# Gated linear attention with a gated MLP: transposes from TensorE to VectorE and DMA, value products on two column halves

## Chip, cores, metric

One core of one Trainium2 chip. The metric is the device time of one execution in microseconds (us), median of three runs.

## The reference, cut to what matters

Two blocks in float32 (the MLP's weights arrive as float64 and are converted on the chip). B = 4, H = 8, S = 768, D = 48; 3072 tokens of 384; the MLP is 2048 wide.

```python
mag = np.sqrt(a_re * a_re + a_im * a_im)
scale = np.minimum(mag, 0.999) / (mag + 1e-06)
a_re_n, a_im_n = (a_re * scale, a_im * scale)
for t in range(S):
    ar, ai = (a_re_n[:, :, t, :, None], a_im_n[:, :, t, :, None])
    new_re = ar * S_re - ai * S_im
    new_im = ar * S_im + ai * S_re
    kv = np.einsum('bhd,bhe->bhde', k[:, :, t], v[:, :, t])
    S_re, S_im = (new_re + kv, new_im)
    y[:, :, t] = np.einsum('bhd,bhde->bhe', q[:, :, t], S_re)
x = y.transpose(0, 2, 1, 3).reshape(B * S, H * D)
h = x @ w_in
return (h * np.cos(h)) @ w_out
```

## The kernel before

The complex gates are turned into magnitudes and angles, both summed along a chunk, so that a chunk's outputs are products of matrices. A chunk is C = 128 tokens of one batch (24 chunks, n), a group is G = 2 chunks (12 groups, g). All of it runs in `fast_path`; `general_path` stands behind a flag computed at the end and is not taken with these inputs.

Per group, on tiles of 128 tokens x 768 (two chunks x 8 heads x 48):

- `g_log` (L627), `g_prod` (L655), `g_angle` (L681): logarithm of the gate's magnitude (`m2`, called m in the trace), its running sum on TensorE (`lgs`, L662), the factors P and Q, and the angle. The last token's row of P goes to DRAM and comes back transposed as `end` (L674 to L675, two DMAs on SP's queue).
- `g_phase` (L693, `phs`), `g_trig` (L706): the running angle, its sine and cosine (`trig`).
- `g_stack` (L715): `ks` and `qs`, keys and queries times cosine and sine, 16 heads x 96 (L722, one VectorE operation of 128x1536 each).

Per chunk:

- `f_transpose` (L727): `kT` and `qT` [96, 8 heads, 128], eight TensorE transposes each (`tp`, L734), copied from PSUM by ScalarE (L736).
- `f_scores` (L738): per head kT x qT (`sc`, L744), multiplied on VectorE with the causal mask into `atm` (L746).
- `f_state` (L763): the chunk's own state, ks x v (`sp`, L769), added to the running `state` [96, 8, 48] by VectorE and GpSimd (L774 to L778); the last chunk of a batch has none.
- `f_out` (L749): `yp` = atm x v (L755) plus state x queries (L758; the first chunk of a batch has no state), tokens on partitions, copied to `x` (L761).
- `f_xt` (L782): x transposed by three TensorE transposes (`xp`, L788) into the group's `xT` (L789).

Per group again: `mm1` (L791), eight calls of twelve records on TensorE for two slices of the width (`hp`, L796), ScalarE and VectorE between (`turn`, `cs`, Sin), and the product `gate` (L807); `mm2` (L810), two calls of 16 matmuls (`op`, L813), then out. In the profile one float32 matmul counts as two records, a transpose as one.

The loop at the end of `fast_path` runs a software pipeline. Iteration `it` does the gates of group `it`, the chunks of `it-1`, `mm1` of `it-2` and `mm2` of `it-3`: first g_log, g_prod, g_angle and mm2, then a weave of the steps of `gates` (spread over the first half), `chunks` and `mm1` (spread over all of it). The Tile framework's scheduler takes this order as priorities, sets the final order on each engine and inserts the waits; buffers come from pools with a fixed number of copies (`bufs`). DMAs issued with `nc.sync` stand on one queue (SP) in order. `special` keeps the ScalarE functions that need a table in the order written, so the logarithms of the next group stand behind the last Sin of mm1.

Of the kernel before, what the change touches and what calls it, by code (L numbers as in the profile page):

```python
# [11 lines left out]
F32 = mybir.dt.float32  # L12
# [5 lines left out]
ALU = mybir.AluOpType  # L18
# [467 lines left out]
def fast_path(ctx, tc, q, k, v, a_re, a_im, moe_w_in, moe_w_out, out, least):  # L486
# [14 lines left out]
    ND = DM // C  # L501
    NJ = DF // C
    assert DM == H * D and NCH % G == 0

# [26 lines left out]
    X = [dict() for _ in range(NG)]  # L531
# [43 lines left out]
    def from_double(dst, src):  # L575
# [24 lines left out]
        nc.vector.scalar_tensor_tensor(out=dst, in0=e, scalar=897.0, in1=dst,  # L600
                                       op0=ALU.is_ge, op1=ALU.mult)

    chained = []

    def chain(ins):
# [18 lines left out]
    def temp(tag, bufs=1):  # L624
        return gt.tile([C, G * DM], F32, tag=tag, name=tag, bufs=bufs)
# [29 lines left out]
    def g_prod(g):  # L655


        x = X[g]
        x["P"], x["Q"] = temp("P"), temp("Q")
        for i in range(G):  # L660
            ps = pa.tile([C, DM], F32, tag="a", name="lgs")
            nc.tensor.matmul(ps, lhsT=sums, rhs=x["lg"][:, ts(i, DM)], start=True, stop=True)  # L662
            special(out=x["P"][:, ts(i, DM)], in_=ps, func=AF.Exp)
            special(out=x["Q"][:, ts(i, DM)], in_=ps, func=AF.Exp, scale=-1.0)
        u = temp("mag")
        nc.vector.scalar_tensor_tensor(out=u, in0=x["Q"], scalar=HUGE, in1=x["P"],
                                       op0=ALU.min, op1=ALU.mult)
        for name in "PQ":
            nc.vector.scalar_tensor_tensor(out=x[name], in0=u, scalar=3.0, in1=x[name],
                                           op0=ALU.subtract, op1=ALU.mult)  # L670
        row = rows_d.tile([G * DM], F32, tag="row", name="row")
        nc.scalar.dma_start(out=row, in_=x["P"][C - 1:C].rearrange("o x -> (o x)"))
        x["end"] = ft.tile([D2, G * H], F32, tag="end", name="end")
        for a in range(2):  # L674
            nc.sync.dma_start(out=x["end"][ds(a * D, D)], in_=row.rearrange("(x d) -> d x", d=D))  # L675
# [29 lines left out]

    def g_trig(g):  # L706
        x = X[g]
        x["trig"] = gt.tile([C, 2, G * DM], F32, tag="trig", name="trig")
        cs, sn = x["trig"][:, 0], x["trig"][:, 1]
        nc.vector.tensor_scalar(out=cs.bitcast(U32), in0=x["ph"].bitcast(U32),  # L710
                                scalar1=0x7FFFFFFF, scalar2=None, op0=ALU.bitwise_and)
        special(out=sn, in_=x["ph"], func=AF.Sin, scale=TWO_PI)
        special(out=cs, in_=cs, func=AF.Sin, scale=-TWO_PI, bias=half_pi_b)

    def g_stack(g):  # L715
        x = X[g]
        nc.gpsimd.tensor_tensor(out=x["P"], in0=flat(x["q"]), in1=x["P"], op=ALU.mult)
        nc.gpsimd.tensor_tensor(out=x["Q"], in0=flat(x["k"]), in1=x["Q"], op=ALU.mult)
        for name, src, eng in (("ks", x["Q"], nc.vector), ("qs", x["P"], nc.vector)):
            t = gt.tile([C, G * H, 2, D], F32, tag=name, name=name, bufs=2)  # L720
            shape = [C, G * H, 2, D]
            eng.tensor_tensor(  # L722
                out=t, in0=src.rearrange("p (x d) -> p x d", d=D).unsqueeze(2).to_broadcast(shape),
                in1=x["trig"].rearrange("p a (x d) -> p x a d", d=D), op=ALU.mult)
            x[name] = t

    def f_transpose(n, name, hh):  # L727
        g, i = divmod(n, G)
        if hh == 0:
            Y[n][name] = ft.tile([D2, H, C], F32, tag=name, name=name)  # L730
        ps = pa.tile([D2, HH, C], F32, tag="a", name="tp")
        for h in range(HH):
            head = i * H + hh * HH + h
            nc.tensor.transpose(ps[:, h], X[g][name[0] + "s"][:, head].rearrange(  # L734
                "p a d -> p (a d)"), ident)
        nc.scalar.copy(out=Y[n][name][:, ts(hh, HH)], in_=ps)  # L736

    def f_scores(n, hh):  # L738
        y = Y[n]
        if hh == 0:  # L740
            y["atm"] = ft.tile([C, H, C], F32, tag="atm", name="atm")
        ps = pa.tile([C, HH, C], F32, tag="a", name="sc")
        for h in range(HH):
            nc.tensor.matmul(ps[:, h], lhsT=y["kT"][:, hh * HH + h], rhs=y["qT"][:, hh * HH + h],  # L744
                             start=True, stop=True)
        nc.vector.tensor_tensor(out=y["atm"][:, ts(hh, HH)], in0=ps,  # L746
                                in1=causal.unsqueeze(1).to_broadcast([C, HH, C]), op=ALU.mult)

    def f_out(n):  # L749
        y, (g, i) = Y[n], divmod(n, G)  # L750
        vals = X[g]["v"][:, i]
        state = y.get("state")
        ps = pa.tile([C, H, D], F32, tag="a", name="yp")
        for h in range(H):
            nc.tensor.matmul(ps[:, h], lhsT=y["atm"][:, h], rhs=vals[:, h],  # L755
                             start=True, stop=(state is None))
            if state is not None:
                nc.tensor.matmul(ps[:, h], lhsT=y["qT"][:, h], rhs=state[:, h],  # L758
                                 start=False, stop=True)
        y["x"] = ft.tile([C, DM], F32, tag="x", name="x")  # L760
        nc.scalar.copy(out=y["x"], in_=ps.rearrange("p h d -> p (h d)"))  # L761

    def f_state(n):  # L763
        if n % NCH == NCH - 1:
            return
        y, (g, i) = Y[n], divmod(n, G)
        ps = pa.tile([D2, H, D], F32, tag="a", name="sp")
        for h in range(H):
            nc.tensor.matmul(ps[:, h], lhsT=X[g]["ks"][:, i * H + h].rearrange("p a d -> p (a d)"),  # L769
                             rhs=X[g]["v"][:, i, h], start=True, stop=True)  # L770
# [11 lines left out]
    def f_xt(n):  # L782
        g, i = divmod(n, G)
        if i == 0:
            X[g]["xT"] = msb.tile([C, ND, G, C], F32, tag="xT", name="xT")
        ps = pa.tile([C, ND, C], F32, tag="a", name="xp")
        for dc in range(ND):
            nc.tensor.transpose(ps[:, dc], Y[n]["x"][:, ts(dc, C)], ident)  # L788
        nc.scalar.copy(out=X[g]["xT"][:, :, i], in_=ps)  # L789

    def mm1(g, jp):  # L791
        x = X[g]
# [136 lines left out]
```

## Time and profile before

| | |
|---|---|
| median of 3 runs | 931.01 us (930.38 to 933.06) |
| the profiled execution | 938.23 us |
| its span | 936.4 us |
| instructions | 10169 |
| TensorE busy | 797.1 us, 85% of the span |
| VectorE busy | 497.1 us, 53% |
| ScalarE busy | 378.6 us, 40% |
| GpSimd busy | 171.3 us, 18% |

How to read the lines shown later. PE is TensorE's matmul stream, PEld its weight loads, DVE is VectorE, ACT ScalarE, POOL GpSimd, SP the engine that issues most DMAs; SPq is its queue. A row of groups gives the line, engine and operation, output and inputs by name, partitions x elements, how many; behind the first bar the busy time in us and the mean of one in ns; behind the second the idle time of the engine just before them and what ended most of it. A row of the chain of waits gives the start, the length and the work, one piece behind the other, each released by the one before. A row of windows gives the stretch, its length, the busy time and count of each engine in it, the granted TensorE clock (1.00 is full speed), the share of the DMA engines, and GB/s. A row of an engine's timeline gives start, length and operation.

### The profile page before, as it was taken

How to read it: one execution, taken by the hardware profiler on the slowest of the kernel's cores; microseconds unless marked ns; L12 is line 12 of the kernel's file. 1: busy time of each engine (PE TensorE's matmuls, PEld its weight loads, DVE VectorE, ACT ScalarE, POOL GpSimd, SP SyncE). 2: the span in 40 equal slices, each digit the busy share in tenths (PEclk: the TensorE clock that was granted, in tenths of full speed). 3: DMA queues.
4: the chain of work that ended last, by engine and by line, in shares of the span. 5: the costliest groups of instructions: out<-in, count | busy, mean ns of one | idle time of the engine just before them, and what ended most of it. 6: DMA issues, size and time to landing. Idle time of an engine off the chain costs nothing.

```text
span 936.4 us, 10169 instructions
## 1 busy us (share of the span) xinstructions
PE 797.1 (85%) x3920; PEld 621.0 (66%) x3920; DVE 497.1 (53%) x761; ACT 378.6 (40%) x588; POOL 171.3 (18%) x96
## 2 busy tenths in 40 slices
PE   1101446899999999999999999999999989999997
PEld 0000245685885977967968858858769668778684
DVE  3999985844544736636545446346456445123160
ACT  5222123535454554454364454354544623123140
POOL 2343333403103022112120031031030211000000
PEclk9999966899899999989899999898999998998999
DMA  8523631303004004004023040040040100000000
GB/s 174 141 90 112 146 108 34 69 18 63 23 18 85 1 18 85 1 17 85 1 43 60 18 83 3 18 85 1 18 84 1 26 10 1 9 9 1 9 8 21
DMA packets 151876, 42.03 MB, mean 45 GB/s; under 512 B 144638, under 2 KB 148222, under 8 KB 151818
## 3 DMA queue, kind: packets, MB, share of 16 engines
q1 hardware_dynamic: 151218, 40.98, 19.8%
q8 instruction: 33, 0.54, 0.3%
q10 hardware_dynamic: 600, 0.30, 0.1%
q14 instruction: 25, 0.20, 0.1%
HBM read 36.51 MB, written 4.76 MB: 44 GB/s over the span
## 4 chain that ended last, share of the span: by engine, by line
PE 70%; ACT 6%; DVE 2%; POOL 2%; DMA 1%; issue 1%; ACTq 0%; SPq 0%; POOLq 0%; DVEq 0%
PE hp L796 28%; PE op L813 17%; PE yp L755 4%; PE sc L744 4%; PE yp L758 4%; PE tp L734 4%; PE sp L769 3%; POOL m L646 2%; ACT rs L619 2%; PE lgs L662 1%; ACT L618 1%; PE phs L697 1%; PE phs L700 1%; PE xp L788 1%; ACT m L619 1%; ACT mag L619 1%
## 5 line engine op out<-in xcount | busy, mean ns | idle before, releaser
L796 PE MATMUL hp<-xT,w_in 128*128 128x256 f32 x1152 | 294.0, 409 | 4.1 <-DVE gate L807 3.5
L796 PEld LDWEIGHTS hp<-xT,w_in 128*128 128x128 f32 x1152 | 231.0, 207 | 39.7 <-DVE gate L807 3.9
L813 PE MATMUL op<-w_out,gate 128*128 128x384 f32 x768 | 251.1, 486 | 0.0
L813 PEld LDWEIGHTS op<-w_out,gate 128*128 128x128 f32 x768 | 145.9, 190 | 99.2
L803 DVE TENSOR_SCALAR cs<-turn 128x512 f32<-128x512 f32 x96 | 42.4, 443 | 172.9 <-ACT turn L802 172.9
L802 ACT ACTIVATE turn<-hp,quarter_b 128x512 f32<-128x512 f32 x96 | 65.7, 685 | 124.6 <-PE hp L796 122.7
L807 DVE TENSOR_TENSOR gate<-hp,cs 128x512 f32<-128x512 f32 x96 | 66.2, 690 | 82.2 <-ACT cs L619 81.4
L776 POOL TENSOR_TENSOR state<-state,end 96x384 f32<-96x384 f32 x16 | 31.2, 1949 | 342.2 <-DVE state L774 179.1
L755 PE MATMUL yp<-v,atm 128*128 128x48 f32 x384 | 75.3, 292 | 19.3 <-DVE atm L746 19.3
L619 ACT ACTIVATE cs<-cs 128x512 f32<-128x512 f32 x96 | 60.5, 630 | 69.0 <-DVE cs L805 69.0
L662 PE MATMUL lgs<-m,sums 128*128 128x384 f32 x48 | 21.3, 572 | 64.6 <-POOL m L646 49.3
L755 PEld LDWEIGHTS yp<-v,atm 128*128 128x128 f32 x384 | 62.0, 209 | 20.4 <-DVE atm L746 20.2
L758 PE MATMUL yp<-state,qT 96*128 96x48 f32 x320 | 67.7, 296 | 0.0
L805 DVE TENSOR_TENSOR cs<-turn,cs 128x512 f32<-128x512 f32 x96 | 65.9, 687 | 2.1
L662 PEld LDWEIGHTS lgs<-m,sums 128*128 128x128 f32 x48 | 9.2, 211 | 75.2 <-POOL m L646 71.3
L646 POOL TENSOR_TENSOR m<-m,rs 128x768 f32<-128x768 f32 x12 | 22.0, 1835 | 197.6 <-ACT rs L619 196.7
L697 PE MATMUL phs<-sq,sums 128*128 128x384 f32 x48 | 22.4, 557 | 38.8 <-DVE sq L688 38.8
L758 PEld LDWEIGHTS yp<-state,qT 96*128 96x128 f32 x320 | 54.2, 212 | 0.0
L761 ACT COPY x<-yp 128x384 f32<-128x384 f32 x24 | 11.5, 478 | 104.6 <-PE yp L758 94.0
L633 ACT ACTIVATE m<-re 128x768 f32<-128x768 f32 x12 | 10.1, 842 | 97.3 <-DMA re<-in_a_re_dram 97.3
L744 PE MATMUL sc<-qT,kT 96*128 96x128 f32 x384 | 48.4, 277 | 0.1
L744 PEld LDWEIGHTS sc<-qT,kT 96*128 96x128 f32 x384 | 46.9, 192 | 2.3 <-ACT qT L736 1.0
(77 smaller groups left out, 955.0 us busy)
## 6 DMA issues: line engine op xcount, KB each, us to landing
raw<-in_moe_w_in_dram SPq DMA_DIRECT2D x12, 512.0 KB
raw<-in_moe_w_out_dram SPq DMA_DIRECT2D x16, 384.0 KB
re<-in_a_re_dram SPq DMA_DIRECT2D x24, 192.0 KB
im<-in_a_im_dram SPq DMA_DIRECT2D x24, 192.0 KB
k<-in_k_dram SPq DMA_DIRECT2D x24, 192.0 KB
q<-in_q_dram SPq DMA_DIRECT2D x24, 192.0 KB
v<-in_v_dram SPq DMA_DIRECT2D x24, 192.0 KB
out_dram<-ot SPq DMA_DIRECT2D x24, 192.0 KB
```

The source lines that it names most:

```text
L619: chain(nc.scalar.activation(func=func, **kw))
L646: nc.gpsimd.tensor_tensor(out=m2, in0=m2, in1=rs, op=ALU.subtract)
L662: nc.tensor.matmul(ps, lhsT=sums, rhs=x["lg"][:, ts(i, DM)], start=True, stop=True)
L744: nc.tensor.matmul(ps[:, h], lhsT=y["kT"][:, hh * HH + h], rhs=y["qT"][:, hh * HH + h], start=True, stop=True)
L755: nc.tensor.matmul(ps[:, h], lhsT=y["atm"][:, h], rhs=vals[:, h], start=True, stop=(state is None))
L758: nc.tensor.matmul(ps[:, h], lhsT=y["qT"][:, h], rhs=state[:, h], start=False, stop=True)
L796: nc.tensor.matmul(ps[:, ji], lhsT=w_in[:, dc, ts(jp * 2 + ji, C)], rhs=x["xT"][:, dc].rearrange("p g t -> p (g t)"), start=(dc == 0), sto ...
L802: nc.scalar.activation(out=turn, in_=ps, func=AF.Identity, scale=INV_TWO_PI, bias=quarter_b)
L803: nc.vector.tensor_scalar(out=cs, in0=turn, scalar1=ROUND, scalar2=ROUND, op0=ALU.add, op1=ALU.subtract)
L805: nc.vector.tensor_tensor(out=cs, in0=turn, in1=cs, op=ALU.subtract)
L807: nc.vector.tensor_tensor(out=gate, in0=ps, in1=cs, op=ALU.mult)
L813: nc.tensor.matmul(ps, lhsT=X[g]["gate"][j // 2][:, j % 2, ts(i, C)], rhs=w_out[:, j], start=(j == 0), stop=(j == NJ - 1))
```

## The change

Four things, and no other arithmetic:

1. Keys and queries are no longer transposed on TensorE. VectorE transposes blocks of 32x32 (`tr` [128, 768], one operation for a chunk's keys, one for its queries, two buffers), and twelve DMAs on SP's queue put the blocks in place: four quarters of the tokens x three blocks of 32 rows, 32 partitions each. This step moves from `chunks(it-1)` to `gates(it)`, an iteration ahead of its use; kT and qT get three buffers. For blocks of 32 the 96 rows of a head are ordered in runs of 16 (cosine and sine alternately), so `ks` and `qs` are made by two VectorE operations of 128x768 each, `trig` lies in two temporaries that the next group uses as well, and `end` comes by six DMAs instead of two.
2. `f_out` computes the transpose of what it computed: v and state are the stationary operand (48 columns), atm and qT move (128 columns). Even heads go to PSUM partitions 0 to 47, odd heads to 64 to 111, in turn. Two ScalarE copies put the result into `yT`.
3. `f_xt` runs once per group: ten DMAs on SP's queue from yT to xT, in place of six TensorE transposes and two ScalarE copies.
4. `cs` shares the buffer of `gate`, of which there are eleven instead of twelve.

```diff
@@ g_prod
-        for a in range(2):
-            nc.sync.dma_start(out=x["end"][ds(a * D, D)], in_=row.rearrange("(x d) -> d x", d=D))
+        for part in range(D2 // R):
+            nc.sync.dma_start(
+                out=x["end"][ds(part * R, R)],
+                in_=row.rearrange("(x b d) -> b d x", d=R, b=NR)[part // 2])
@@ g_trig
-        x["trig"] = gt.tile([C, 2, G * DM], F32, tag="trig", name="trig")
-        cs, sn = x["trig"][:, 0], x["trig"][:, 1]
+        cs, sn = x["trig"] = temp("rs"), temp("mag")
@@ g_stack
+            t = gt.tile([C, G * H * NR, 2, R], F32, tag=name, name=name,
+                        bufs=2 if name == "ks" else 1)
+            for a in range(2):
+                nc.vector.tensor_tensor(
+                    out=t[:, :, a], in0=src.rearrange("p (x d) -> p x d", d=R),
+                    in1=x["trig"][a].rearrange("p (x d) -> p x d", d=R), op=ALU.mult)
@@ f_transpose
-        ps = pa.tile([D2, HH, C], F32, tag="a", name="tp")
-        for h in range(HH):
-            head = i * H + hh * HH + h
-            nc.tensor.transpose(ps[:, h], X[g][name[0] + "s"][:, head].rearrange(
-                "p a d -> p (a d)"), ident)
-        nc.scalar.copy(out=Y[n][name][:, ts(hh, HH)], in_=ps)
+        tr = ft.tile([C, NR, H, 32], F32, tag="tr", name="tr")
+        nc.vector.transpose(out=tr, in_=X[g][name[0] + "s"][:, ts(i, H * NR)].rearrange(
+            "p (h b) a d -> p b h (a d)", b=NR))
+        if name == "kT":
+            t = Y[n][name] = ft.tile([D2, H, Q4, 32], F32, tag=name, name=name, bufs=3)
+            place = t.rearrange("p h q j -> p q h j")
+        else:
+            t = Y[n][name] = place = ft.tile([D2, Q4, H, 32], F32, tag=name, name=name, bufs=3)
+        for a in range(Q4):
+            for b in range(NR):
+                nc.sync.dma_start(out=place[ts(b, 32), a], in_=tr[ts(a, 32), b])
@@ f_out
-        ps = pa.tile([C, H, D], F32, tag="a", name="yp")
-        for h in range(H):
-            nc.tensor.matmul(ps[:, h], lhsT=y["atm"][:, h], rhs=vals[:, h],
-                             start=True, stop=(state is None))
+        ps = pa.tile([C, HH, C], F32, tag="a", name="yp")
+        for p in range(HH):
+            for side in range(2):
+                nc.tensor.matmul(ps[ds(side * 64, D), p], lhsT=vals[:, 2 * p + side],
+                                 rhs=y["atm"][:, 2 * p + side], start=True, stop=(state is None))
             if state is not None:
-                nc.tensor.matmul(ps[:, h], lhsT=y["qT"][:, h], rhs=state[:, h],
-                                 start=False, stop=True)
-        y["x"] = ft.tile([C, DM], F32, tag="x", name="x")
-        nc.scalar.copy(out=y["x"], in_=ps.rearrange("p h d -> p (h d)"))
+                for side in range(2):
+                    nc.tensor.matmul(ps[ds(side * 64, D), p], lhsT=state[:, 2 * p + side],
+                                     rhs=queries(y, 2 * p + side), start=False, stop=True)
+        for side in range(2):
+            half = ds(side * 64, D)
+            nc.scalar.copy(out=X[g]["yT"][half, :, i], in_=ps[half])
@@ f_xt
-        ps = pa.tile([C, ND, C], F32, tag="a", name="xp")
-        for dc in range(ND):
-            nc.tensor.transpose(ps[:, dc], Y[n]["x"][:, ts(dc, C)], ident)
-        nc.scalar.copy(out=X[g]["xT"][:, :, i], in_=ps)
+        for h in range(H):
+            row = h * D
+            while row < (h + 1) * D:
+                n = min((h + 1) * D, (row // C + 1) * C) - row
+                nc.sync.dma_start(out=xt[ds(row % C, n), row // C],
+                                  in_=X[g]["yT"][ds(h % 2 * 64 + row - h * D, n), h // 2])
+                row += n
@@ mm1
-        cs = msb.tile([C, 2, G * C], F32, tag="cs", name="cs")
-        gate = msb.tile([C, 2, G * C], F32, tag="gate", name="gate", bufs=12)
+        gate = msb.tile([C, 2, G * C], F32, tag="gate", name="gate", bufs=11)
+        cs = gate
@@ gates
+        for i in range(G):
+            for name in ("kT", "qT"):
+                yield lambda i=i, name=name: f_transpose(g * G + i, name)
@@ chunks
-            for name in ("kT", "qT"):
-                for hh in range(2):
-                    yield lambda n=n, name=name, hh=hh: f_transpose(n, name, hh)
...
-            yield lambda n=n: f_xt(n)
+            if n == ns[-1]:
+                yield lambda: f_xt(g)
```

The new line numbers: hp L817, op L834, sc L758, sp L789, yp L772 (values) and L776 (state), tr L738, the DMAs of kT and qT L747, of xT L808, of end L679.

TensorE's order around the second chunk of a group, before (a program's matmul is one row here):

```order
L796 MATMUL hp<-xT,w_in 128x256 x6
L788 MATMUL xp<-ident,x 128x128 x3
L734 MATMUL tp<-ident,ks 96x128 x8
L796 MATMUL hp<-xT,w_in 128x256 x6
L734 MATMUL tp<-ident,qs 96x128 x8
L796 MATMUL hp<-xT,w_in 128x256 x6
L744 MATMUL sc<-qT,kT 128x128 x8
L796 MATMUL hp<-xT,w_in 128x256 x6
L769 MATMUL sp<-v,ks 96x48 x8
L755 MATMUL yp<-v,atm 128x48
L758 MATMUL yp<-state,qT 128x48
```

The same place now:

```order
L758 MATMUL sc<-qT,kT 128x128 x4
L817 MATMUL hp<-xT,w_in 128x256 x6
L758 MATMUL sc<-qT,kT 128x128 x4
L817 MATMUL hp<-xT,w_in 128x256 x6
L789 MATMUL sp<-v,ks 96x48 x8
L817 MATMUL hp<-xT,w_in 128x256 x6
L772 MATMUL yp<-atm,v 48x128 x2
L776 MATMUL yp<-qT,state 48x128 x2
```

The tp and xp are gone, and the sp, which stood directly ahead of yp, has a block of hp behind it now.

SP's queue over one group in the steady part of the loop, before:

```order
L541 DMA re<-in_a_re_dram 128x8x48
L675 DMA end<-row 48x16x1 x2
L541 DMA re<-in_a_re_dram 128x8x48
L541 DMA k<-in_k_dram 128x8x48
L541 DMA q<-in_q_dram 128x8x48 x2
L817 DMA out_dram<-ot 128x384
L541 DMA v<-in_v_dram 128x8x48 x2
```

And now:

```order
L544 DMA q<-in_q_dram 128x8x48 x2
L747 DMA kT<-tr 32x8x32 x12
L747 DMA qT<-tr 32x256 x12
L747 DMA kT<-tr 32x8x32 x12
L747 DMA qT<-tr 32x256 x12
L808 DMA xT<-yT 48x256 x2
L808 DMA xT<-yT 32x256
L808 DMA xT<-yT 16x256
L808 DMA xT<-yT 48x256 x2
L808 DMA xT<-yT 16x256
L808 DMA xT<-yT 32x256
L808 DMA xT<-yT 48x256 x2
```

The 48 DMAs of the next group's kT and qT stand ahead of the ten that make this group's xT.

VectorE's order in the start-up now, from the last part of the weight conversion (L603) on; the tr up to here are group 0's and group 1's:

```order
L603 SCALAR_TENSOR_TENSOR w_out<-t,w_out 128x384
L738 STREAM_TRANSPOSE tr<-qs 128x768
L760 TENSOR_TENSOR atm<-sc,causal 128x512 x2
L793 SCALAR_TENSOR_TENSOR state<-sp,state 96x384
L639 TENSOR_TENSOR m_824<-m_824,sq 128x768
L644 TENSOR_TENSOR mag<-mag,sq 128x768
L645 TENSOR_SCALAR m_824<-m_824 128x768
L738 STREAM_TRANSPOSE tr<-ks 128x768
L653 SCALAR_TENSOR_TENSOR sq<-mag,sq 128x768
L655 SCALAR_TENSOR_TENSOR sq<-sq,im 128x768
L670 SCALAR_TENSOR_TENSOR mag<-Q,P 128x768
L673 SCALAR_TENSOR_TENSOR P<-mag,P 128x768
```

Two more operations of g_prod follow, with the last transpose of group 1 between them: what belongs to group 2's gates (L639 to L673) stands among group 1's transposes.

More of the change, by code (lines that the diff above doesn't have):

```diff
@@ L501, in fast_path @@
     ND = DM // C
+    R = 16
+    NR = D // R
+    Q4 = C // 32
     NJ = DF // C
@@ L718, in g_stack, with f_transpose, queries @@
         nc.gpsimd.tensor_tensor(out=x["Q"], in0=flat(x["k"]), in1=x["Q"], op=ALU.mult)
[L719 to L724, printed above, removed]
+        for name, src in (("ks", x["Q"]), ("qs", x["P"])):
+            t = gt.tile([C, G * H * NR, 2, R], F32, tag=name, name=name,
[4 more added lines that the diff above has]
+                    in1=x["trig"][a].rearrange("p (x d) -> p x d", d=R), op=ALU.mult)
             x[name] = t
-    def f_transpose(n, name, hh):
+    def f_transpose(n, name):
         g, i = divmod(n, G)
-        if hh == 0:
-            Y[n][name] = ft.tile([D2, H, C], F32, tag=name, name=name)
-        ps = pa.tile([D2, HH, C], F32, tag="a", name="tp")
-        for h in range(HH):
-            head = i * H + hh * HH + h
-            nc.tensor.transpose(ps[:, h], X[g][name[0] + "s"][:, head].rearrange(
-                "p a d -> p (a d)"), ident)
-        nc.scalar.copy(out=Y[n][name][:, ts(hh, HH)], in_=ps)
+        tr = ft.tile([C, NR, H, 32], F32, tag="tr", name="tr")
[9 more added lines that the diff above has]
+                nc.sync.dma_start(out=place[ts(b, 32), a], in_=tr[ts(a, 32), b])
+    def queries(y, h):
+        return y["qT"][:, :, h]
     def f_scores(n, hh):
@@ L768, in f_state @@
         for h in range(H):
-            nc.tensor.matmul(ps[:, h], lhsT=X[g]["ks"][:, i * H + h].rearrange("p a d -> p (a d)"),
-                             rhs=X[g]["v"][:, i, h], start=True, stop=True)
+            keys = X[g]["ks"][:, ts(i * H + h, NR)].rearrange("p b a d -> p (b a d)")
+            nc.tensor.matmul(ps[:, h], lhsT=keys, rhs=X[g]["v"][:, i, h], start=True, stop=True)
         new = ft.tile([D2, H, D], F32, tag="state", name="state")
@@ L780, in f_state, with f_xt @@
         Y[n + 1]["state"] = new
[L782 to L785, printed above, removed]
-        ps = pa.tile([C, ND, C], F32, tag="a", name="xp")
-        for dc in range(ND):
-            nc.tensor.transpose(ps[:, dc], Y[n]["x"][:, ts(dc, C)], ident)
-        nc.scalar.copy(out=X[g]["xT"][:, :, i], in_=ps)
+    def f_xt(g):
+        xt = X[g]["xT"] = msb.tile([C, ND, G, C], F32, tag="xT", name="xT")
+        for h in range(H):
[5 more added lines that the diff above has]
+                row += n
     def mm1(g, jp):
```

4 lines of the change are left out of this document (3 added, 1 removed).

## The prediction

> **What bounds the kernel now.** First the page's totals, its chain by engine, and one stretch from the first op (L813) to the last op's end beside the stretch before it.
>
> ```profile
> span 936.4 us, 10169 instructions
> PE 797.1 (85%) x3920; PEld 621.0 (66%) x3920; DVE 497.1 (53%) x761; ACT 378.6 (40%) x588; POOL 171.3 (18%) x96
> PE 70%; ACT 6%; DVE 2%; POOL 2%; DMA 1%; issue 1%; ACTq 0%; SPq 0%; POOLq 0%; DVEq 0%
> ```
> ```profile
> core 0: us, PE busy (x) PEld busy (x) DVE busy (x) ACT busy (x) POOL busy (x), PEclk, DMA share, GB/s
> 0.00:209.40 209.40, 89.35 (x447) 71.50 (x448) 158.06 (x265) 68.12 (x98) 70.64 (x47) 0.89 0.41 99
> 209.40:930.45 721.05, 707.79 (x3474) 549.53 (x3472) 339.06 (x496) 309.98 (x489) 100.69 (x49) 0.96 0.14 29
> 482.14:544.70 62.56, 61.37 (x323) 48.06 (x323) 33.95 (x49) 31.37 (x49) 9.52 (x6) 1.00 0.20 39
> 544.70:614.07 69.37, 68.18 (x338) 53.63 (x338) 34.04 (x49) 31.31 (x49) 12.45 (x7) 0.93 0.17 35
> ```
> From 209.4 to 930.45 PE is busy for 707.79 of 721.05 us: PE is the bound there, and what is taken off it comes off the time. Before 209.4 VectorE is the busiest (158.06 of 209.4, most of it converting weights). The granted clock is 0.96 in the long stretch, so about 0.04 x 721 = 29 us are lost to it. The last two rows are two groups with the same kinds of work: one at clock 1.00, the other at 0.93 and 6.8 us longer.
>
> Then the places where the clock goes: the chain of waits around two chunks, and windows cut at its pieces.
>
> ```profile
> 443.53 1.32 PE sp L769 x16
> 444.85 0.22 PE yp L755 x2
> 445.07 0.22 PE yp L758 x2
> ...
> 509.84 1.32 PE sp L769 x16
> 511.16 1.79 PE yp L755 x16
> ```
> ```profile
> 443.53:447.40 3.87, 3.87 (x41) 3.87 (x40) 3.54 (x5) 0.80 (x2) 0.85 (x1) 0.98 0.01 4
> 447.40:449.40 2.00, 2.00 (x11) 2.00 (x11) 1.28 (x1) 0.01 (x1) 1.97 (x1) 0.50 0.00 0
> 449.40:451.00 1.60, 1.60 (x5) 1.24 (x6) 0.57 (x1) 1.00 (x2) 0.00 (x0) 0.50 0.00 0
> ...
> 509.84:512.95 3.11, 3.11 (x33) 3.11 (x33) 2.78 (x4) 0.80 (x2) 0.00 (x0) 1.00 0.00 0
> 512.95:515.00 2.05, 2.05 (x10) 1.80 (x10) 2.05 (x3) 1.07 (x2) 0.00 (x0) 1.00 0.00 0
> ```
> At 443.53 the products of 48 moving columns begin, sp and then sixteen yp in one run; 3.9 us later the clock is 0.50, though PE is busy in every microsecond. At 509.84 the chunk has no state, the run of such products ends after 3.11 us, and the clock stays at 1.00. So it is not idle time that halves the clock here but a long run of thin products. The Trainium skill ("TensorE: Matmul & The Clock Gate", what's actually happening) gives half rate after an idle window of about 3.4 us. By that rule nothing in this change would touch the 29 us and the sum below would be 25 us smaller; the trace, halved with PE busy 2.00 of 2.00 us, speaks against idleness as the cause.
>
> **The change part by part.** I count from the first op on, where ten of the twelve groups still have their chunk work to do, and against the profiled run (936.4 plus 1.8 around it = 938.23 us, 7.2 above the median of 931.01).
>
> *Transposes off PE.* The rows are pieces of the chain at full clock.
>
> ```profile
> 454.42 0.33 PE xp L788 x3
> 454.75 0.87 PE tp L734 x8
> ...
> 439.15 1.79 PE sc L744 x16
> ```
> A tp takes 0.87/8 = 0.109 us; ten groups have 320: -34.9 us. An xp takes 0.11, ten groups have 60: -6.5. The ACT copies of both (L736, L789) go too, but ACT is busy 31 of 62 to 69 us per group, so that counts nothing.
>
> *Value and state products.* Before, a product is 0.22 us for a pair of records with the whole array as weights and 48 columns moving. Now 48 columns are the weights, 128 move, and two neighbours stand in different column halves. The ten groups have 160 value and 136 state products: 296 x 0.2235 = 66.2 us. No row shows two halves at work together. If they overlap fully, half goes: -33.1. If they don't, a product costs what another one with 128 moving columns does, sc: 1.79/8 = 0.224 us, thus no gain, with some loss for changing the array's form. I take the overlap, as independent outputs on separate columns have nothing in common but the moving side, less 0.25 us at each of the 20 chunks for the change of form, 5 us, an estimate of the size of one product's time: -28. Ends: -33 and +5. The Trainium skill ("TensorEngine Tiling (Array Packing)", Key Properties) says that tiles run in parallel and that a change of tiling mode drains the array; no row here shows either.
>
> *The clock.* sp and yp now have a hp of 2.6 us at full rate between them, and yp's run is shorter and moves 128 columns, as sc does at clock 1.00. I take 25 of the 29 us as regained; ends 0 and 29.
>
> *What comes instead: VectorE.* Four 32x32 transposes of 128x768 per group. The trace has none; the nearest row has the same shape, and ks and qs (L722) are split into ops of half the size.
>
> ```profile
> L635 DVE TENSOR_TENSOR m<-m,sq 128x768 f32<-128x768 f32 x12 | 11.4, 948 | 7.2 <-ACT sq L634 7.2
> L722 DVE TENSOR_TENSOR qs<-P,trig 128x1536 f32<-128x1536 f32 x12 | 22.1, 1839 | 0.0
> L813 PE MATMUL op<-w_out,gate 128*128 128x384 f32 x768 | 251.1, 486 | 0.0
> ```
> 0.95 us each, 3.8 per group: VectorE goes from 34.0 to 37.8 us of a group that I expect to last 65.6 - 9 = 57. Of that, some 30 lie in the 36 us beside hp and the chunks, since the op stretch (64 records, 20.6 us) leaves VectorE little to do. VectorE isn't the bound, but near it: hp waits for a gate (L807) more often. I take 0.6 us a group, +6; ends 0 and 15.
>
> *What comes instead: SP.* A group has 48 DMAs of kT and qT, 10 of xT and 4 more of end: 62 in place of none. SP's own timeline has the prices, and the chain a landing.
>
> ```profile
> 401.05 0.99 SPq L541 DMA_DIRECT2D v<-in_v_dram  x2
> 421.61 0.37 SPq L817 DMA_DIRECT2D out_dram<-ot  x1
> 426.55 1.34 SPq L675 DMA_DIRECT2D end<-row  x2
> ```
> ```profile
> 749.85 2.27 DMA end<-row
> ```
> 0.37 to 0.67 us of issue each; eight may be in flight, so landings of 2.27 allow one per 0.28 (the program makes each DMA on SP wait for the eighth before it). At 0.45, as for the 128-row loads, 62 take 28 us, beside 6.5 for the rest: 34 of 57, no bound. Three things queue behind them. xT's ten are behind the 48 on SP, but the next hp comes only after the op's 20.6 us, which covers them. VectorE's third transpose needs the buffer of the first, its fourth that of the second (tr has two): the second's twelve DMAs have landed 24 x 0.45 + 2.3 = 13.1 us after the first transpose, and by the order of the instructions about 22 others, some 15 us, stand between the first and the fourth, so no wait. And v and re of later groups follow; they have a period to spare. I count nothing, and 3 us a group where a DMA takes 0.67.
>
> *Start-up.* Group 1's last transpose now stands on VectorE behind g_log and g_prod of group 2, and the xT of group 0 on SP behind its DMAs.
>
> ```profile
> 149.69 0.56 DVE L600 SCALAR_TENSOR_TENSOR w_out<-t,w_out 128x384 f32<-128x384 uint32 x1 [0.29 <-POOL w_out L596]
> ```
> ```profile
> 156.01 6.38 PE L796 MATMUL hp<-xT,w_in 128*128 128x256 f32 x18 [0.57 <-ACT xT L789]
> ```
> The first hp comes 6.3 us after the last weight, and I expect it at about 186 rather than 156. But group 1's chunk work is then done while PE is idle anyway, so the 53 us from first hp to first op become about 27: op starts near 213 instead of 209.4. +4; ends 0 and 15.
>
> Sum: -34.9 - 6.5 - 28 - 25 + 6 + 4 = -84.4, so 853.8 for the profiled run and 931.0 - 84.4 = 847 for the median.
>
> **The rivals.** *The halves don't overlap.* Then the yp term is +5 instead of -28: 847 + 33 = 880. For it: nothing in this trace shows two products at once. Against: nothing shared but the moving side.
>
> *The half clock stays*, with or without the runs of thin products: -84.4 + 25 gives 872. For it: yp still fills only half of the array's columns with weights. Against: sp is now apart from yp, and sc moves 128 columns at 1.00.
>
> *VectorE becomes the bound beside hp.* Transposes of twice 0.95 us, or SP at 0.67 us a DMA, which makes the fourth transpose wait about 3 us: 3 to 4 us per group, 10 groups, 877 to 885. For it: 30 of 36 us are taken. Against: no 128x768 row is far over 0.95.
>
> *SP sets the pace (slower).* Op starts near 213, 62 us follow the last chunk (868.4 to 930.5 before) and 1.8 lie around the span; between them are ten periods. They equal 938.2 where a period is 66.1, that is (66.1 - 6.5)/62 = 0.96 us per DMA. At 1.05 they last 71.6 each: 213 + 716 + 62 + 2 = 993, or 985 on the median; at 1.0, 955. I take 960. For it: the DMAs go from SBUF to SBUF, 32 partitions and for kT 256 runs of 128 bytes each, a kind that no row shows. Against: 768 runs of 4 bytes (end) took 0.67. The Trainium skill ("DMA: Bandwidth & Descriptors", Rules for kernel authors) says that under 64 KB mostly overhead is paid; each of the 48 moves 32 KB.
>
> *The change gains nothing*, because a new wait of hp, for xT or a gate, takes just what PE was given back: 931.
>
> **How the numbers follow.** Chances: forecast 0.50 (847; 832 to 862 by its own ends), halves without overlap 0.22 (880), half clock stays 0.10 (872), VectorE bound 0.08 (881), SP bound 0.07 (960), no gain 0.03. The low end takes full overlap, full clock and no new waits, 847 - 5 - 4 - 10 = 828. The high end takes in the middle three, with a few us of VectorE's waits on top of the 880: 890. That leaves out about 0.15. Some 0.3% (2.8 us) can be told from no change here: faster 0.90, same 0.03, slower 0.07.
>
> **What would show it right or wrong.** Right: a granted clock near 1.00 from the first op on; a pair of yp products in the time of one; a transpose near 0.95 us; SP idle at some point in each group; lgs to lgs in 56 to 58 us. Wrong: yp products 0.22 us apart in the chain (halves in turn), PEclk below 0.98 after the first op, hp waiting for xT with SP issuing up to that point, or VectorE's transposes waiting for DMAs. If periods are over 66 us, the forecast's sign is wrong.

## The result, and the profile after

The changed kernel takes 846.26 us (845.57 to 846.55, four runs) against 932.03 us (930.38 to 935.01) of the kernel before on the same chip: 0.9075 of its time, 95% interval 0.905 to 0.910. Its profiled execution took 846.44 us, with a span of 844.6.

First the page's totals, its row of granted clock in 40 slices and its chain by engine:

```profile
span 844.6 us, 10236 instructions
PE 682.8 (81%) x3464; PEld 506.9 (60%) x3464; DVE 526.6 (62%) x833; ACT 338.8 (40%) x492; POOL 152.3 (18%) x96
PEclk9999975579999999999999999999999999999999
PE 56%; DVE 15%; SPq 9%; ACT 8%; POOL 6%; issue 3%; DMA 3%; DVEq 0%; POOLq 0%; ACTq 0%
```

TensorE has 114 us less to do, no slice after the start-up is below 9, and SP's queue and VectorE now have a part in the chain. Then windows: up to the first op, from there to the end of the last, and three groups from lgs to lgs.

```profile
0.00:219.15 219.15, 74.26 (x370) 54.59 (x371) 160.22 (x281) 60.36 (x81) 64.97 (x47) 0.84 0.48 112
219.15:838.70 619.55, 608.53 (x3095) 452.31 (x3093) 366.39 (x553) 277.94 (x410) 87.37 (x49) 1.00 0.33 66
...
285.13:340.71 55.58, 54.51 (x283) 40.88 (x283) 36.80 (x55) 28.23 (x41) 8.85 (x6) 1.00 0.43 85
340.71:397.82 57.11, 56.04 (x301) 42.15 (x301) 37.17 (x55) 28.22 (x41) 10.40 (x7) 1.00 0.39 79
397.82:453.61 55.79, 54.65 (x285) 40.78 (x285) 36.53 (x54) 27.96 (x41) 9.19 (x6) 1.00 0.40 78
```

The long stretch shrank from 721.05 to 619.55 us, by 101.5, at a clock of 1.00 instead of 0.96; the first op comes 9.75 us later than before (209.4). A group takes 55.6 to 57.1 us, all but 1.1 of it with TensorE busy. The chain around one chunk's value products:

```profile
253.32 2.66 PE hp L817 x12
255.98 0.36 PE yp L772 x4
256.33 0.22 PE yp L776 x4
256.55 0.22 PE yp L772 x4
256.77 0.22 PE yp L776 x4
256.99 0.22 PE yp L772 x4
257.21 0.22 PE yp L776 x4
257.44 0.22 PE yp L772 x4
257.65 0.22 PE yp L776 x4
257.88 2.79 PE hp L817 x12
```

Two products of two records each take 0.22 us, what one took before. Sixteen last 1.90 us (16 x 0.2235 = 3.58 before); the first pair costs 0.14 more than the others, and the hp behind them 0.13 more than the hp behind sp. Last, the groups of the new operations on VectorE, and SP's queue over one group:

```profile
L738 DVE STREAM_TRANSPOSE tr<-ks 128x768 f32<-128x768 f32 x24 | 23.3, 970 | 0.0
L738 DVE STREAM_TRANSPOSE tr<-qs 128x768 f32<-128x768 f32 x24 | 23.1, 964 | 0.0
```
```profile
369.80 7.88 SPq L747 DMA_DIRECT2D kT<-tr  x12
377.78 8.16 SPq L747 DMA_DIRECT2D qT<-tr  x12
386.05 7.82 SPq L747 DMA_DIRECT2D kT<-tr  x12
393.98 7.53 SPq L747 DMA_DIRECT2D qT<-tr  x12
401.61 6.25 SPq L808 DMA_DIRECT2D xT<-yT  x10
407.96 1.15 SPq L544 DMA_DIRECT2D v<-in_v_dram  x2
409.21 3.23 SPq L679 DMA_DIRECT2D end<-row  x6
```

A transpose takes 0.97 us. A DMA of keys or queries takes SP 0.65 us, and SP is occupied for 7.9 + 8.2 + 7.8 + 7.5 + 6.3 + 1.2 + 3.2 and some 8 for the loads and stores, 50 of 57 us.

### The profile page after: what moved, and what is told of

Same layout as the page of the kernel before. It is cut to its first block, busy times and chain, and to the rows that moved or that the text cites. A ratio compares the mean times of both kernels' runs of the same rounds, so it can differ in the third digit from the quotient of the medians.

```text
span 844.6 us, 10236 instructions
## 1 busy us (share of the span) xinstructions
PE 682.8 (81%) x3464; PEld 506.9 (60%) x3464; DVE 526.6 (62%) x833; ACT 338.8 (40%) x492; POOL 152.3 (18%) x96
## 4 chain that ended last, share of the span: by engine, by line
PE 56%; DVE 15%; SPq 9%; ACT 8%; POOL 6%; issue 3%; DMA 3%; DVEq 0%; POOLq 0%; ACTq 0%
PE hp L817 23%; PE op L834 18%; SPq L747 7%; PE sc L758 4%; PE sp L789 2%; POOL m L650 2%; PE yp L772 2%; POOL w_out L599 2%; PE lgs L666 2%; ACT rs L623 2%; PE phs L703 2%; PE yp L776 2%; PE phs L706 1%; DVE gate L826 1%; ACT L622 1%
## 5 line engine op out<-in xcount | busy, mean ns | idle before, releaser
L817 PE MATMUL hp<-xT,w_in 128*128 128x256 f32 x1152 | 267.5, 385 | 4.3 <-DVE gate L828 3.7
L834 PE MATMUL op<-w_out,gate 128*128 128x384 f32 x768 | 251.1, 486 | 0.0
L817 PEld LDWEIGHTS hp<-xT,w_in 128*128 128x128 f32 x1152 | 214.8, 192 | 36.8 <-DVE gate L828 4.1
L834 PEld LDWEIGHTS op<-w_out,gate 128*128 128x128 f32 x768 | 145.9, 190 | 99.2
L623 ACT ACTIVATE gate<-gate 128x512 f32<-128x512 f32 x96 | 60.1, 627 | 91.6 <-DVE gate L826 89.8
L828 DVE TENSOR_TENSOR gate<-hp,gate 128x512 f32<-128x512 f32 x96 | 65.4, 685 | 37.1 <-ACT gate L623 35.2
L824 DVE TENSOR_SCALAR gate<-turn 128x512 f32<-128x512 f32 x96 | 40.3, 420 | 75.7 <-ACT turn L823 74.5
L826 DVE TENSOR_TENSOR gate<-turn,gate 128x512 f32<-128x512 f32 x96 | 65.5, 685 | 1.7
L795 POOL TENSOR_TENSOR state<-state,end 96x384 f32<-96x384 f32 x16 | 16.4, 1023 | 263.1 <-DVE state L793 166.7
L758 PEld LDWEIGHTS sc<-qT,kT 96*128 96x128 f32 x384 | 51.7, 201 | 16.4 <-issue 10.4
L758 PE MATMUL sc<-qT,kT 96*128 96x128 f32 x384 | 52.4, 286 | 8.2 <-DMA qT<-tr 8.2
L703 PE MATMUL phs<-sq,sums 128*128 128x384 f32 x48 | 22.4, 556 | 43.5 <-DVE sq L694 43.5
L772 PE MATMUL yp<-atm,v 128*48 128x128 f32 x384 | 39.4, 289 | 21.2 <-DVE atm L760 21.2
L760 DVE TENSOR_TENSOR atm<-sc,causal 128x512 f32<-128x512 f32 x48 | 32.7, 682 | 20.6 <-PE sc L758 20.6
L772 PEld LDWEIGHTS yp<-atm,v 128*48 128x48 f32 x384 | 23.0, 128 | 30.2 <-issue 24.9
```

Source lines behind the costliest of these rows:

```text
L623: chain(nc.scalar.activation(func=func, **kw))
L703: nc.tensor.matmul(ps, lhsT=sums, rhs=x["turn"][:, ts(i, DM)], start=True, stop=first)
L772: nc.tensor.matmul(ps[ds(side * 64, D), p], lhsT=vals[:, 2 * p + side], rhs=y["atm"][:, 2 * p + side], start=True, stop=(state is None))
L817: nc.tensor.matmul(ps[:, ji], lhsT=w_in[:, dc, ts(jp * 2 + ji, C)], rhs=x["xT"][:, dc].rearrange("p g t -> p (g t)"), start=(dc == 0), sto ...
L826: nc.vector.tensor_tensor(out=cs, in0=turn, in1=cs, op=ALU.subtract)
L828: nc.vector.tensor_tensor(out=gate, in0=ps, in1=cs, op=ALU.mult)
```

## The experiments

The theory: after the first op TensorE sets the time, and it gained in three ways, by the transposes that it no longer does, by two value products at a time, and by a clock that no longer halves. The rivals: the products got short for another reason than their neighbours; the clock recovered because TensorE's transposes are gone, not because the thin runs are; VectorE or SP took something back after the first op.

### e1_sides: are the halves at work together only as neighbours?

```diff
-        for p in range(HH):
-            for side in range(2):
-                nc.tensor.matmul(...lhsT=vals[:, 2 * p + side]...)
-            if state is not None:
-                for side in range(2):
-                    nc.tensor.matmul(...lhsT=state[:, 2 * p + side]...)
+        for side in range(2):
+            for p in range(HH):
+                nc.tensor.matmul(...lhsT=vals[:, 2 * p + side]...)
+                if state is not None:
+                    nc.tensor.matmul(...lhsT=state[:, 2 * p + side]...)
```

> The changed kernel with its value and state products written side after side: the four even heads first, then the four odd ones, so that neighbours on TensorE stand in the same column half. Theory (two halves work at once only if they are neighbours): each product takes its own 0.22 us again, 296 x 0.11 = 33 us less the first pair's overhead, so 846 + 31 = 877, with the clock still at 1.00 after the first op. Rival (48 columns of weights make a product short, whatever is beside it): 846, no change.

869.93 us (869.53 to 871.25); 643.0 us from the first op to the last instead of 619.5, at clock 1.00. The chain of one chunk's products:

```profile
255.42 0.35 PE yp L772 x2
255.77 0.22 PE yp L775 x2
255.99 0.22 PE yp L772 x2
256.21 0.22 PE yp L775 x2
256.43 0.22 PE yp L772 x2
256.65 0.22 PE yp L775 x2
256.87 0.26 PE yp L772 x4
257.13 0.22 PE yp L775 x4
```

One product per 0.22 us again, and two pairs (x4) where the order passes from one side to the other. So the halves work at once, and only neighbours do. The expected 31 us were too many by those two pairs: 14 pieces stand in place of 8, 6 x 0.22 = 1.3 us a chunk with state and half of it in the three without, 24.4 us over twenty chunks against 23.5 measured.

### e2_out_only and e3_keys_only: the change in two parts

e2 is the kernel before with f_out, f_xt and the shared gate buffer of the change, and its own transposes. e3 is the changed kernel with the old f_out and f_xt; the queries are laid out as the keys are:

```diff
-        if name == "kT":
-            t = Y[n][name] = ft.tile([D2, H, Q4, 32], ...)
-            place = t.rearrange("p h q j -> p q h j")
-        else:
-            t = Y[n][name] = place = ft.tile([D2, Q4, H, 32], ...)
+        t = Y[n][name] = ft.tile([D2, H, Q4, 32], ...)
+        place = t.rearrange("p h q j -> p q h j")
```

> The kernel before with only the value side changed: column halves, yT and the ten DMAs to xT; keys and queries are still transposed on TensorE. Theory (the clock is halved by long runs of thin products, sp and yp): the run is now at most 1.3 + 1.9 us, the clock is near 1.00 after the first op; yp -30, xp -6.5, clock -22 to -29, start-up as before: 931 - 62 = 869 (865 to 873). Rival (TensorE's transposes have a part in it): the clock stays at 0.96 and the time is 891 to 895.

> The changed kernel with the value side of before: yp with 48 moving columns, the x copy and the xp transposes; keys and queries by VectorE and DMA (the queries laid out as the keys are, so that they can be weights: 256 runs of 128 bytes in a DMA instead of 32). Theory (only the length of the thin run counts): yp's run of 3.6 us stands apart from sp, between the 3.1 us that kept the clock and the 4.9 that halved it; -35 for tp, +10 for the start-up, and the clock's loss somewhere from 0 to 29: 884 to 906. Rival (TensorE's transposes lower the clock): 1.00 after the first op, 884 or less.

e2: 867.37 us (866.45 to 869.50), clock 1.00 after the first op. e3: 890.22 us (886.04 to 893.61), 0.97. Windows of both from the first op to the last:

```profile
201.91:860.31 658.40, 645.85 (x3415) 487.36 (x3413) 339.31 (x496) 317.49 (x489) 87.93 (x49) 1.00 0.18 39
```
```profile
208.33:885.86 677.53, 668.69 (x3159) 509.93 (x3158) 371.15 (x557) 273.28 (x411) 86.46 (x50) 0.97 0.31 56
```

e2 keeps TensorE's transposes and has a full clock; e3 has none and loses some. So the transposes are not what halves it. The two parts save 67 and 44 us of the 934 measured beside them, together 111, and the whole change 86. From the first op to the last they save 62.7 and 43.5, together 106.2 against 101.5, so only 4.7 us are counted twice there, as e3 regains some of the clock too (it is at 0.50 for 44 us, the kernel before for 61). The rest is mainly the start-up: the first op comes 7.5 and 1.1 us earlier in the parts, and 9.75 later in the whole. In e3 a run of yp stands alone, and its clock halves in some groups only. The timeline and windows show one:

```profile
452.53 0.42 PE L766 MATMUL yp<-v,atm 128*128 128x48 f32 x2 [1.28 <-DVE atm L757]
452.79 0.39 PE L769 MATMUL yp<-state,qT 96*128 96x48 f32 x2
```
```profile
450.70:452.53 1.83, 0.56 (x4) 0.15 (x2) 1.34 (x3) 0.46 (x1) 0.00 (x0) 1.00 0.33 120
452.53:454.40 1.87, 1.87 (x17) 1.87 (x17) 1.87 (x3) 0.00 (x0) 0.00 (x0) 1.00 0.00 0
454.40:457.68 3.28, 3.28 (x19) 3.28 (x17) 3.10 (x4) 0.00 (x0) 0.00 (x0) 0.51 0.06 10
```

TensorE waits 1.28 us for atm and does thin products for 1.87 us; then the clock is 0.51. Idle time and thin products count together here. In another group yp comes without a wait, 3.6 us from 246.21 on, and halves the clock by itself:

```profile
246.24:249.65 3.41, 3.41 (x33) 3.41 (x31) 1.74 (x3) 0.91 (x2) 0.32 (x1) 1.00 0.34 53
249.65:253.06 3.41, 3.41 (x11) 2.79 (x11) 0.69 (x1) 1.49 (x3) 0.00 (x0) 0.50 0.62 115
```

### e4_sp_first: the clock by order alone

```diff
+            yield lambda n=n: f_state(n)
             for hh in range(2):
                 yield lambda n=n, hh=hh: f_scores(n, hh)
-            yield lambda n=n: f_state(n)
             yield lambda n=n: f_out(n)
```

> The kernel before, with the state's products (sp) written ahead of the scores, so that sp and yp no longer follow each other; nothing else. Theory (the run of 4.9 us of thin products halves the clock, 3.6 don't): the granted clock rises from 0.96 towards 1.00 after the first op and the time falls by up to 22 us, to 909. Rival (yp alone is enough, or TensorE's transposes are the cause): 931, the clock 0.96 as before.

908.24 us (907.64 to 908.52), 0.974 of the kernel before (0.968 to 0.979). The scheduler also put hp into the middle of yp, so no run of 48 moving columns is longer than 1.8 us. The window from the first op to the last:

```profile
208.84:900.69 691.85, 678.72 (x3475) 527.52 (x3473) 339.08 (x496) 312.57 (x489) 89.58 (x49) 1.00 0.15 30
```

The same work as in the kernel before, 29.2 us shorter, at clock 1.00 but for one stretch of 3.41 us behind a wait for VectorE (at 744.2). That is the clock's whole price, and it takes the move of one line to get it.

### e11_out_sides: thin products or long runs?

e2 with the edit of e1.

> The kernel with only the value side changed, its products written side after side, so that sp and yp form a run of 1.3 + 3.3 = 4.6 us in one chunk of two. Theory (it is products of 48 moving columns that halve the clock when they follow each other for 3.9 us or more): yp moves 128 columns, the clock stays at 1.00 after the first op, and the time is that kernel's 867 plus 24: 891. Rival (any such run of short products that leaves most of the array's columns without weights or work halves it): clock 0.95 to 0.97, 905 to 915.

895.86 us (895.59 to 896.17). No stretch of 10 us between the first op and the last is below clock 1.00. A run of sp and sixteen products with 128 moving columns, all but two pairs of them single, takes 4.6 us and keeps the clock; what halves it is the 48 moving columns. The profiled run is 26 us longer than that of e2: 3.7 are the start-up (the first op at 205.6 instead of 201.9); from the first op to the last it takes 22.6 us longer, where 24 were expected.

### e5_twice: VectorE's slack

```diff
+        nc.vector.transpose(out=tr, in_=X[g][name[0] + "s"][:, ts(i, H * NR)].rearrange(
+            "p (h b) a d -> p b h (a d)", b=NR))
```

> The changed kernel with every VectorE transpose done twice into the same tile: 3.9 us more of VectorE per group, 37 to 41 of some 56 us, all else alike. Theory (after the first op VectorE has slack beside TensorE's work; a group lasts what TensorE needs): the groups stay at 55.6 to 57.1 us but for a few tenths, the start-up, where VectorE is full, grows by 4 to 8 us: 850 to 856. Rival (VectorE is level with TensorE beside hp): 3.9 us more per group, ten groups, 885 to 890.

851.96 us (851.30 to 852.39), 5.7 more for 38 us of work on VectorE. The first op comes at 220.75 instead of 219.15, and groups take 55.1 to 57.7 us. The four more transposes cost 0.4 us a group on the average of eight groups; the rival's 3.9 did not show.

### e6_dmas96: SP's price and where it becomes the bound

The kernel has the new loop once for kT (L749) and once for qT (L752); it is shown once.

```diff
-                nc.sync.dma_start(out=place[ts(b, 32), a], in_=tr[ts(a, 32), b])
+                for u in range(2):
+                    nc.sync.dma_start(out=place[ts(b, 32), a, ts(u, H // 2)],
+                                      in_=tr[ts(a, 32), b, ts(u, H // 2)])
```

> The changed kernel with each of the 48 DMAs of a group's keys and queries cut in two (same bytes): 110 instead of 62 on SP's queue. Theory (a DMA costs SP some 0.65 us whatever its size, and SP becomes the bound above a group's TensorE time): 110 x 0.65 + 6.5 = 78 us a group instead of 56, 22 x 10 more and 20 more in the start-up: about 1085, slower than the kernel before. Rival (the cost goes with the bytes): 0.4 us each, 50 us a group, SP still hidden: 846 to 860.

1186.0 us (1185.3 to 1189.1), 1.274 of the kernel before (1.265 to 1.284). SP's queue in one group, and two groups by windows:

```profile
444.86 15.46 SPq L749 DMA_DIRECT2D kT<-tr  x24
460.41 15.12 SPq L752 DMA_DIRECT2D qT<-tr  x24
```
```profile
352.39:441.50 89.11, 66.07 (x285) 48.48 (x285) 37.42 (x55) 27.96 (x41) 8.52 (x6) 0.81 0.26 50
441.50:528.35 86.85, 67.73 (x301) 49.37 (x301) 37.42 (x55) 27.96 (x41) 9.35 (x7) 0.83 0.26 50
```

A DMA of half the bytes costs SP 0.64 us, as a whole one does: the price is per DMA. 96 are 61 us and the rest of the queue 18, together 79, near the 78 expected. On top of that SP waits some 6 to 7 us for a transpose, and a group takes 86 on the average. TensorE now waits for qT (179 us in all), and in these groups its clock falls to 0.81 to 0.83. The sign of the expectation held, its size did not: 30 us more a group instead of 22, and a first op at 258.1, 39 us later instead of 20. For a group, what the expectation left out is SP's own wait.

### e7_actq and e8_poolq: another queue for the queries

```diff
-                nc.sync.dma_start(out=place[ts(b, 32), a], in_=tr[ts(a, 32), b])
+                (nc.sync if name == "kT" else nc.scalar).dma_start(
+                    out=place[ts(b, 32), a], in_=tr[ts(a, 32), b])
```

e8 has nc.gpsimd in place of nc.scalar.

> The changed kernel with the queries' 24 DMAs of a group issued on ScalarE's queue, the keys' 24 left on SP's. Theory (the ten to seventeen us by which the first op comes later than without these DMAs are SP's queue; later groups hide it): the first op comes at 205 to 212 instead of 219, the groups stay at 56 us: 833 to 840. Rival (ScalarE's own work waits behind 24 issues of 0.65 us, 15.6 us a group, and the chain that runs from the last gate to lgs goes over ScalarE): 2 us or more per group, 860 to 870.

> The changed kernel with the queries' 24 DMAs of a group issued by GpSimd, which is busy for 9 of 56 us a group; the keys' 24 stay on SP's queue. Theory: as with ScalarE's queue, the first op at 205 to 212, 833 to 840. Rival (GpSimd takes over 1 us for each of these, and the state's product and m stand behind them on it): 24 us a group more on GpSimd, the wait ahead of lgs grows from 1.1 us to several, 860 or more.

e7: 957.37 us (956.56 to 958.95), slower than the kernel before. ScalarE's own timeline and the waits of TensorE say why:

```profile
420.93 8.35 ACTq L747 DMA_DIRECT2D qT<-tr  x12
429.32 1.15 ACT L623 ACTIVATE gate<-gate 128x512 f32<-128x512 f32 x2 [8.62 <-DMA qT<-tr]
```
```profile
PE hp L818 <- DVE gate L829: 63.9, 18, 8.0
```

Twelve issues block ScalarE for 8.35 us, the Sin of a gate stands behind them, and hp waits for that gate. The rival was right and too small: groups take 67.6 us on the average of five. The first op came no earlier either (230.7).

e8: 841.55 us in the middle of four runs, three of them from 839.84 to 841.68; the fourth took 4097 us, for which no profile gives a reason. The first op comes at 213.3 instead of 219.2 and GpSimd is busy for 21 instead of 9 us per group, without harm to the groups. That is the theory, with a first op and a time just outside what it expected (205 to 212, 833 to 840).

### e9_first2 and e10_first3: TensorE's transposes where TensorE is idle

```diff
+        if g < 2:
+            ...
+            for hh in range(2):
+                ps = pa.tile([D2, HH, Q4, 32], F32, tag="a", name="tp")
+                for h in range(HH):
+                    head = i * H + hh * HH + h
+                    nc.tensor.transpose(ps[:, h]..., X[g][name[0] + "s"][:, ts(head, NR)]..., ident)
+                nc.scalar.copy(out=place[:, ts(hh, HH)], in_=ps)
+            return
         tr = ft.tile([C, NR, H, 32], F32, tag="tr", name="tr")
```

e10 has g < 3.

> The changed kernel with the keys and queries of groups 0 and 1 transposed on TensorE, as before, into the new places; groups 2 to 11 by VectorE and DMA. Theory (in the start-up TensorE is idle and VectorE and SP are full, so there the change costs what it later gains): the first op comes at 202 to 208 instead of 219, the groups stay at 56 us: 829 to 836. Rival (the start-up's extra time comes from the value side's DMAs and waits, or group 2's 48 DMAs, which also come ahead of the first op, hold it as much): 842 to 846.

> The same with the first three groups on TensorE: group 2's transposes stand beside the first hp. Theory: TensorE has 3.5 us more there, but no gate waits behind a transpose that waits for DMAs, so the first op comes where it did without these DMAs, near 202: 828 to 832. Rival (TensorE is the bound from the first hp on): 3.5 us later than with two groups.

e9: 829.95 us (829.27 to 831.59), 0.890 of the kernel before (0.886 to 0.895) and 16 us under the changed kernel; the first op comes at 202.6. It beats both kernels. e10: 834.15 us (833.16 to 834.93), 4.2 more than e9 (3.5 expected of the rival): the first op comes at 205.9. That is the rival: TensorE is busy for 3.6 us more (691.3 instead of 687.7), and the 32 transposes of one more group are paid in full.

### e12_before: the spread of the kernel before

> The kernel before, unchanged, profiled once more. Its executions spread from 924 to 937 us, those of the changed kernel by 1 us. Theory (what differs from one to the next is how many of the thin runs halve the clock): from first to last op, the length times the missing clock accounts for the difference to the first profile (721 us at 0.96) within 2 us, and TensorE's busy time at full clock, some 692 us with its idle 13, is the same. Rival: DMA or start-up times vary instead, at the same clock.

933.35 us in the middle of eight runs from 923.59 to 936.18; its profiled execution took 933.75, 4.5 less than the first profile. From the first op to the last it took 717.8 us instead of 721.05, and e4 takes 691.85 for the same work at full clock: 26 us lost here, 29 there. The start-up differs by 1.3 us. The trace's own clock settles the rest. After the first op the first profile is at 0.50 in eleven stretches, 61.4 us in all, and this one in ten, 54.6 us: at half rate the 6.8 us between them cost 3.4, and 3.25 were measured. The executions without a trace fit this, as e1, e4 and the changed kernel, at full clock, spread by 1 to 2 us.

Why the number varies can be read from where these stretches begin. Each lasts 3.41 or 6.83 us, and their starts (249.30, 334.64, 399.49 and so on) lie whole multiples of 3.413 us apart, as on a fixed grid. Ten of the thirteen runs of sp and yp, 4.9 us each, fill a slot of the grid or nearly so, and the clock is halved behind it. The other three (at 376.3, 527.1 and 724.7) lie across two slots, fill neither, and the clock is 1.00 in them and behind them. The eleventh stretch follows a wait of 2.5 us for VectorE (phs, at 764.5).

## Why the prediction came out, step by step

The median forecast, 847, was within 1 us. The sum behind it was less exact: it gave 853.8 us for a profiled run, and that took 846.4. The forecast took the saving of a profiled run that lost more to the clock than most and put it on the median, 7 us lower; measured on the profiles the saving is 91.8 us, on the medians 85.8. The two errors cancel, and that the median was met so closely is luck.

- *Transposes off TensorE*, -34.9 and -6.5: from e2 to the changed kernel the stretch from the first op shrinks by 38.9, of which 37.3 is busy time. Held within 4 us. What goes beyond the 34.9 is a wait of 2.38 us for VectorE in e2 (phs, up to 711.15) and the 3.41 us at clock 0.50 that go with it, 1.7 us; the changed kernel has neither.
- *Value products*, -28 with an estimate of 0.25 us a chunk for the change of form: from e4 to e2 value products and xp together give -33.5 against -34.5 forecast. The change of form costs 0.14 us ahead and 0.13 behind. e1 shows the overlap itself.
- *Clock*, -25 of 29: all of it, 29.2 by e4. The reason given, long runs of 48 moving columns, holds: e4 breaks the runs and e11 widens the columns, both at 1.00, and e2 and e3 exclude TensorE's transposes.
- *VectorE*, +6: nothing. The price of a transpose was right (0.97 us measured, 0.95 forecast) and so was the load (36.8 of 56 us, 37.8 forecast), but after the first op TensorE waits for no gate, and its idle time is the wait ahead of lgs as before (10.4 us in all, 10.7 before).
- *SP*, nothing: held in the time, not in the size. 0.65 us a DMA instead of 0.45 (the loads' own row, 0.99 for two, gives 0.50), and 50 us a group instead of 34. The margin is 6 to 7 us a group, not 23, and e6 goes over the edge. The slower rival's mechanism was real; its threshold, 0.96 us per DMA, had been worked out with 6.5 us for the rest of the queue, which takes some 10.
- *Start-up*, +4: 9.75, mis-sized as VectorE's term was, the other way. The prediction named two delays, VectorE's order and xT's place behind the DMAs on SP, and put the first hp at 186 without a working; it came at 189.0. The step that failed is that SP's queue was not priced there, for from 149.3 on it sets the first hp alone:

```profile
149.33 7.83 SPq L747 DMA_DIRECT2D kT<-tr  x12
157.26 7.53 SPq L747 DMA_DIRECT2D qT<-tr  x12
164.90 7.82 SPq L747 DMA_DIRECT2D kT<-tr  x12
172.82 7.52 SPq L747 DMA_DIRECT2D qT<-tr  x12
180.39 0.58 SPq L544 DMA_DIRECT2D q<-in_q_dram  x1
181.08 7.73 SPq L808 DMA_DIRECT2D xT<-yT  x10
```

  SP issues without a pause, and xT, whose yT was ready by 160.5, stands behind group 1's 48. VectorE's transposes hold up none of these rows: the last ends at 171.1, ahead of its DMAs' turn at 172.8. From the first hp to the first op it took 30 us where 27 were forecast; 3.7 of them are a wait for a gate, and the clock there was 0.89.

  Neither part of the change does this by itself. e3 has the 48 DMAs and makes xT on TensorE: its first hp comes at 146.8, its first op at 208.3, 1.1 us earlier than before. e2 has xT's DMAs without the 48: 201.9. So the start-up pays for the two on one queue; e8, with half of the 48 elsewhere (213.3), and e9, without them in the first two groups (202.6), agree.

With the measured terms: -29.2 - 33.5 - 38.9 + 9.75 = -91.8, the difference of the two spans (936.4 to 844.6).

## What to carry to other kernels

Moving work off the engine that is the bound pays where that engine is the bound and can cost where it isn't: e9, which leaves TensorE's transposes in the start-up, has the gain with a first op 16.5 us earlier. Before DMAs that the next work waits for are put on a queue, look at what stands ahead of them there (xT behind the 48); another order on SP's queue was not tried. Ahead of a change that adds many small DMAs, price the issuing queue by its own rows and sum all of the queue, not only the new part; and do not put such issues on an engine whose own work is waited for (e7). Where the granted clock dips while TensorE is busy, look at what runs there, and try the order first (e4).

## What the runs showed of the hardware

- Products with 48 moving columns count towards a halved clock as idle time does. The clock was 0.50 in stretches that begin on a grid of 3.413 us. It was halved behind a slot of the grid filled with such products (sp and yp, or the 3.6 us of yp alone in e3), or with 1.3 us of waiting and 1.9 us of them; runs of 4.9 us that lay across two slots kept 1.00 (three of thirteen), as did runs of 1.8 us, and 4.6 us of which 3.3 moved 128 columns. In e6, where TensorE idles, the clock fell to 0.81 to 0.83. The Trainium skill ("TensorE: Matmul & The Clock Gate", what's actually happening) ties the half rate to idle windows of about 3.4 us; e6 agrees with it, and here a window part idle and part thin, or all thin, was enough.
- Two products on different column halves run at once only as neighbours: 0.22 us a pair, 0.22 us each when the same half follows itself (e1). A change between whole array and halves cost 0.14 and 0.13 us. The Trainium skill ("TensorEngine Tiling (Array Packing)", Key Properties) has both the parallel tiles and the drain; the trace agrees with the first, and the two costs fit a drain of that size.
- A DMA from SBUF to SBUF cost SP 0.64 to 0.65 us, whether 32 or 16 KB, and ScalarE 0.70 us (8.35 us for twelve).
